# Attention in steps of two pairs, with PSUM tiles of one purpose each

## Chip, cores and metric

The kernel runs on one core of one Trainium2 chip. The metric is the device time of one execution in microseconds (us), as the median of several runs.

## What is computed

The reference is an attention with a window and a few sink positions, followed by two dense layers that keep the name "moe" from their source:

```python
scores = scale * q @ k.T                      # batch 2, 8 heads, 768 positions, 64 wide
keep = (pos_k < n_sink) | (0 <= pos_q - pos_k < window)       # n_sink 4, window 128
a = softmax(where(keep, scores, -1e9))
x = (a @ v), heads side by side               # 1536 rows x 512
h = maximum(x @ moe_w_in, 0);  y = (h * h) @ moe_w_out        # 512 -> 2048 -> 512
h = y @ moe2_w_in
out = (h * tanh(log1p(exp(h)))) @ moe2_w_out
```

## The kernel before, in words

**Tiles.** The 768 positions of each batch are cut into 6 tiles of 128 queries (12 tiles in all, numbered over both batches), and the 8 heads into 4 pairs. The unit of work is a pair of a tile: 48 pairs, numbered 0 to 47. The two heads of a pair (e = 0, 1) lie in partitions 0 to 63 and 64 to 127 of the transposed q and k. A tile with i >= 2 within its batch looks at 208 keys (`WIN`): each half of its query rows (64 rows, index h or r) has its own window of keys, and 16 sink keys (`SK`) are copied between the keys for that purpose by POOL (`sink_keys`, L334). Tile 0 of a batch uses 128 keys, tile 1 uses 256.

**Stages of a pair.** `prep` (L315) transposes q or k of a whole tile on TensorE (4 transposes of 128x128, shown as tr) into a PSUM tile of pool `ps_p`; DVE copies q to `qt`, ACT copies k to `kt`. `emit_s` (L365) computes the scores (s) of one pair, each head into a PSUM bank of its own from `ps_s`. `emit_max` (L380) adds the mask in place on DVE and takes the extreme of each row, one head at a time. `emit_exp` (L389) is the exponential on ACT with the row sums, from PSUM into the probability tile `pr`. `emit_rs` (L401) forms the reciprocals of the sums of two pairs on DVE (L407, L408), and `emit_norm` (L412) multiplies on POOL. `emit_t` (L418) transposes the probabilities of two pairs on TensorE (pt), 16 transposes of 64-row halves, into two banks of `ps_p`, one for each half of the rows; `evac_t` (L436) copies one bank at a time to `pts`, bank 0 on ACT and bank 1 on DVE. `emit_av` (L450) multiplies with v (av). `emit_x` (L477) copies a finished tile from PSUM on ACT, POOL rounds it to a high part (L481) and subtracts for the low part (L483); for the last two tiles DVE subtracts (`split_x`, L490).

**PSUM.** The eight banks: four for `ps_s`, three for `ps_p` (tr and pt alike), one for `ps_a` (av).

**Order.** The order of the work on each engine is written out by hand: the loop at L549 walks n from -3 to 52, one pair a turn. In turn n the scores and maxes of pair n+4, the exponentials of pair n+3, in even turns the reciprocals and normalisation of pairs n+2 and n+3, a `prep` of tile t+2 and the products of pairs n-4 and n-3, in odd turns the transposes of pairs n-1 and n are issued. SP issues all loads of the stage: a tile's q, k, v and `vx` (v rows of the shifted windows and of the sinks, `load_rest`, L292) are loaded three or four tiles ahead when j = 3. `PLAN` (L497) says in which turn which operation of the first three weight blocks is issued (a block is loaded, its words turned into 32-bit floats by ACT (head) and DVE (mid), and split into a high and a low part), and `IN_AT` (L503) when the first two input products of layer one are issued. A short prologue before the loop works on tile 0 in halves, with dummy matmuls (`keep_warm`, L527, shown as idle) on TensorE between.

**After the attention** the function `moe` (L615) runs both layers for all rows, in slots of 12 input matmuls (h) and 12 output matmuls (o, L634), with weight blocks converted on the way.

The lines that set the order around the change are these:

```python
        for n in range(-3, NPR + 5):
            at = {d: pairs[n + d] for d in range(-4, 5) if 0 <= n + d < NPR}
...
            if 4 in at and n > -3:
                emit_s(*at[4])
            if 3 in at and n > -3:
                emit_exp(*at[3])
```

## Time and profile before

| | |
|---|---|
| median of 3 runs | 620.19 us (619.1 to 620.61) |
| the profiled execution | 619.7 us |
| its span, first to last instruction | 617.9 us |
| TensorE matmul busy (PE) | 609.0 us, 99% of the span |
| weight loads (PEld) | 494.5 us, beside the matmuls |
| VectorE (DVE) | 454.5 us, 74% |
| ScalarE (ACT) | 351.0 us, 57% |
| GpSimd (POOL) | 70.1 us, 11%, all in the attention |
| granted TensorE clock, mean | 1.000 of full speed |
| first output matmul of the layers | at 95.80 us |

The shares are means over two very different stages: an attention of some 95 us in which all engines and the DMA engines work, and some 522 us of large matmuls. Names in the rows are those of the program's tiles; "out<-in" says what an instruction writes and reads, and a number in square brackets is idle time of the engine ahead of the instruction with what ended it.

### The profile page before, as it was taken

Reading aid. Unit: us, or ns where it says so; the run is one execution under the profiler, and the core shown is the slowest. Engines: PE = TensorE matmul, PEld = TensorE weight load, DVE = VectorE, ACT = ScalarE, POOL = GpSimd, SP = SyncE. Lnnn points to the kernel's source line nnn. Section 1 sums busy time; section 2 is a strip of 40 time slices with the busy share of each in tenths; the row PEclk is TensorE's granted clock in tenths of the full one; section 3 lists DMA queues with packets and bytes.
Section 4 is the critical chain, followed back from the end, with each engine's and each line's share of the span. In section 5 each row is a group of like instructions: output and inputs, shape, how many; then the busy total and the mean of one; then the engine's idle time right before and its main releaser. Section 6 shows DMA issues by size and latency. Waiting matters only on the chain.

```text
span 617.9 us, 10113 instructions
## 1 busy us (share of the span) xinstructions
PE 609.0 (99%) x3774; PEld 494.5 (80%) x3774; DVE 454.5 (74%) x951; ACT 351.0 (57%) x723; POOL 70.1 (11%) x101
## 2 busy tenths in 40 slices
PE   9999999999999999999999999999999999999996
PEld 6676677888888888888888888888888888888885
DVE  5897889998921111169898789999887788887784
ACT  4888876777743233367777655555444444454442
POOL 5788870000000000000000000000000000000000
PEclk9999999999999999999999999999999999999999
DMA  9998835666600000026666400000010000010001
GB/s 190 198 191 173 185 102 185 207 201 201 198 7 1 0 2 1 1 90 186 190 186 199 137 0 2 1 0 1 1 69 0 1 0 1 28 42 1 1 0 72
DMA packets 74904, 50.24 MB, mean 81 GB/s; under 512 B 52708, under 2 KB 69348, under 8 KB 74852
## 3 DMA queue, kind: packets, MB, share of 16 engines
q1 hardware_dynamic: 74560, 49.16, 29.0%
q8 instruction: 31, 0.51, 0.4%
q10 hardware_dynamic: 292, 0.39, 0.2%
q14 instruction: 21, 0.17, 0.1%
HBM read 46.40 MB, written 3.15 MB: 80 GB/s over the span
## 4 chain that ended last, share of the span: by engine, by line
PE 96%; DVE 2%; ACT 1%; issue 0%; DVEq 0%; ACTq 0%
PE o L634 42%; PE h L195 41%; PE s L373 4%; PE av L465 3%; PE tr L323 2%; PE pt L428 2%; PE idle L529 1%; DVE cv_a L148 0%; DVE cv_r L142 0%; ACT pr L396 0%; DVE cv_r L136 0%; DVE pts L443 0%; DVE qt L329 0%; DVE s L384 0%; DVE rs L408 0%
## 5 line engine op out<-in xcount | busy, mean ns | idle before, releaser
L195 PE MATMUL h<-xh,wil 128*128 128x512 f32 x384 | 102.9, 390 | 0.0
L195 PE MATMUL h<-xl,wih 128*128 128x512 f32 x384 | 102.6, 389 | 0.0
L195 PE MATMUL h<-xh,wih 128*128 128x512 f32 x384 | 102.6, 389 | 0.0
L209 DVE TENSOR_TENSOR gl<-h,gh 128x512 fp32r<-128x512 f32 x48 | 33.2, 691 | 89.3 <-ACT gh L206 89.3
L195 PEld LDWEIGHTS h<-xl,wih 128*128 128x128 f32 x384 | 72.1, 188 | 15.0
L195 PEld LDWEIGHTS h<-xh,wih 128*128 128x128 f32 x384 | 72.1, 188 | 15.0
L195 PEld LDWEIGHTS h<-xh,wil 128*128 128x128 f32 x384 | 71.9, 188 | 14.9
L634 PE MATMUL o<-gh,wol 128*128 128x512 f32 x192 | 74.8, 389 | 0.8 <-DVE wol L171 0.8
L702 ACT ACTIVATE e<-t,small 128x512 f32<-128x512 f32 x48 | 34.8, 725 | 70.7 <-DVE t L698 70.7
L634 PE MATMUL o<-gl,woh 128*128 128x512 f32 x192 | 74.7, 389 | 0.0
L634 PE MATMUL o<-gh,woh 128*128 128x512 f32 x192 | 74.7, 389 | 0.0
L204 ACT ACTIVATE h<-h 128x512 f32<-128x512 f32 x48 | 27.9, 582 | 77.5 <-PE h L195 77.5
L634 PE MATMUL o<-wol,gh 128*128 128x512 f32 x176 | 68.5, 389 | 0.0
L634 PE MATMUL o<-woh,gl 128*128 128x512 f32 x176 | 68.5, 389 | 0.0
L634 PE MATMUL o<-woh,gh 128*128 128x512 f32 x176 | 68.5, 389 | 0.0
L718 ACT CAST gh<-t 128x512 fp32r<-128x512 f32 x44 | 27.4, 623 | 46.1 <-PE o L634 42.7
L148 DVE SCALAR_TENSOR_TENSOR cv_a<-cv_a,cv_r 128x512 int32<-128x512 int32 x64 | 45.2, 706 | 6.2
L209 DVE TENSOR_TENSOR gl<-t,gh 128x512 fp32r<-128x512 f32 x44 | 30.4, 690 | 19.5 <-ACT gh L718 19.5
L396 ACT ACTIVATE pr<-s,nm 128x208 f32<-128x208 f32 (+2 forms) x96 | 40.5, 436 | 6.1 <-DVE nm L384 5.7
L416 POOL TENSOR_TENSOR pr<-pr,rs 128x416 f32<-128x416 f32 (+2 forms) x48 | 41.5, 885 | 15.0 <-DVE rs L408 10.4
L128 ACT ACTIVATE cv_a<-raw 128x512 f32<-128x512 f32 x63 | 42.4, 675 | 0.4 <-DMA raw<-in_moe_w_in_dram 0.2
L634 PEld LDWEIGHTS o<-gh,wol 128*128 128x128 f32 x192 | 36.0, 188 | 8.2 <-PE av L465 0.9
(100 smaller groups left out, 1004.1 us busy)
## 6 DMA issues: line engine op xcount, KB each, us to landing
raw<-in_moe_w_in_dram SPq DMA_DIRECT2D x32, 512.0 KB, 4.0
raw<-in_moe_w_out_dram SPq DMA_DIRECT2D x32, 512.0 KB, 4.3
vn<-in_v_dram SPq DMA_DIRECT2D x12, 256.0 KB, 5.1
qn<-in_q_dram SPq DMA_DIRECT2D x10, 256.0 KB, 4.4
kn<-in_k_dram SPq DMA_DIRECT2D x9, 256.0 KB, 4.8
vx<-in_v_dram SPq DMA_DIRECT2D x16, 128.0 KB, 4.3
out_dram<-ob SPq DMA_DIRECT2D x8, 256.0 KB, 2.4
kn<-in_k_dram SPq DMA_DIRECT2D x6, 128.0 KB, 3.0
```

The source lines that it names most:

```text
L128: nc.scalar.activation(out=self.a, in_=high_words, func=AF.Copy, scale=2.0**-112)
L148: nc.vector.scalar_tensor_tensor(out=ai, in0=ai, scalar=3, in1=self.r, op0=ALU.logical_shift_left, op1=ALU.bitwise_or)
L195: nc.tensor.matmul(ph, lhsT=w[a][:, d, :], rhs=x[:, d, :], start=(m == 0 and d == 0), stop=(m == 2 and d == NDC - 1),)
L204: nc.scalar.activation(out=ph, in_=ph, func=AF.Relu)
L209: nc.vector.tensor_tensor(out=gl, in0=x, in1=f32(gh), op=ALU.subtract)
L373: nc.tensor.matmul(banks[e][qs, 0:w], lhsT=qt[b, i][r, j, qs], rhs=kt[r, j, k0 : k0 + w], start=True, stop=True, skip_group_check=True,)
L396: nc.scalar.activation(out=pr[b, i][:, 2 * j + e, 0:w], in_=banks[e][:, 0:w], func=AF.Exp, bias=nm[:, e : e + 1], scale=-1.0, accum_out=sm ...
L416: nc.gpsimd.tensor_tensor(out=x, in0=x, in1=rs.to_broadcast([P, 2, w]), op=ALU.mult)
L465: nc.tensor.matmul(av[b, i][e * D : (e + 1) * D, j, qs], lhsT=x[0:kv, 2 * j + e, :], rhs=pts[0:kv, c, e, qs], start=(j == 0 and m == 0), s ...
L634: nc.tensor.matmul(acc[sp][t], lhsT=a, rhs=x, start=(fb == 0 and m == 0), stop=(fb == NFB - 1 and m == 2),)
L702: nc.scalar.activation(out=e, in_=t, func=AF.Ln, bias=two)
L718: nc.scalar.copy(g_tiles(n)[0], et[n][1])
```

## The change

The loop goes in steps of two pairs (n even, -2 to 52). The order within a step is written anew.

- PSUM: three banks for `ps_s`, two for the new pool `ps_t` (q and k transposes), two for `ps_p` (one tile, both row halves of pt), one for `ps_a`.
- The scores of two pairs share two banks: head e of both pairs in bank e, 256 columns each. The maxes and the exponentials go head by head: bank 0 for both pairs, then bank 1.
- `prep_rows` transposes q or k in halves of 64 rows, the halves into a bank each, issued directly ahead of pt; `place_rows` copies both, q and k alike, on DVE in the next step. The prologue and tile 1 keep `prep`.
- `evac_t` copies both banks of pt in one ACT instruction. `emit_x` copies on DVE, and POOL takes the low part of every tile.
- The first half of the rows takes its probabilities as columns 0 to 127 and 128 to 255 instead of 0 to 127 and 80 to 207, with v and `vx` rows to match: `vx` is 80 rows high and loaded by four transfers instead of five. The probability tiles are two fixed tiles whose columns from 208 on POOL zeroes at the start.
- k has four buffers instead of three and is loaded and transposed a tile earlier; loads are issued at j = 2. `PLAN` and `SINKS` are moved to even turns.

```diff
-    ps_s = att.enter_context(tc.tile_pool(name="ps_s", bufs=4, space=PSUM, reuse_waits="tile"))
-    ps_p = att.enter_context(tc.tile_pool(name="ps_p", bufs=3, space=PSUM, reuse_waits="tile"))
+    ps_s = att.enter_context(tc.tile_pool(name="ps_s", bufs=3, space=PSUM, reuse_waits="tile"))
+    ps_p = att.enter_context(tc.tile_pool(name="ps_p", bufs=1, space=PSUM, reuse_waits="tile"))
+    ps_t = att.enter_context(tc.tile_pool(name="ps_t", bufs=1, space=PSUM, reuse_waits="tile"))
...
+    def prep_rows(t, which):
+        if t >= len(tiles):
+            return
+        b, i = tiles[t]
+        src = (qn if which == "q" else kn)[b, i]
+        free = ps_t.tile([P, 2, 512], F32, tag="tr", name="tr")[:, :, 0 : 2 * P]
+        free = free.rearrange("p r (j q) -> p r j q", j=NPAIR)
+        for j in range(NPAIR):
+            for r in range(2):
+                rows = slice(r * HQ, (r + 1) * HQ)
+                nc.tensor.transpose(
+                    free[:, r, j, :], src[rows, 2 * j : 2 * j + 2, :].rearrange("p h d -> p (h d)"),
+                    ident[rows, rows],
+                )
+        if which == "q":
+            qt[b, i] = apool.tile([P, NPAIR, P], F32, tag="qt", name="qt", bufs=2)
+            dst = qt[b, i]
+        else:
+            dst = kt[:, :, kpos(i) : kpos(i) + P]
+        st["rows"] = (dst.rearrange("p j (r q) -> p j r q", r=2), free.rearrange("p r j q -> p j r q"))
+
+    def place_rows():
+        if "rows" in st:
+            nc.vector.tensor_copy(*st.pop("rows"))
+
...
-        return ((0, KV), (0, KV))
+        return ((0, P), (0, KV))
...
-    pr = {}
-
-    def emit_s(b, i, j):
+
+    def emit_s(b, i, j, banks):
         c0, w, _ = geom(i)
-        banks = [ps_s.tile([P, 512], F32, tag="s", name="s") for e in range(2)]
...
-    def emit_exp(b, i, j):
+    prs = [apool.tile([P, H, 2 * P], F32, name=f"pr{k}") for k in range(2)]
+    pr = {p: prs[m % 2] for m, p in enumerate(tiles)}
+
+    def emit_exp(b, i, j, heads=(0, 1)):
         w = geom(i)[1]
-        banks, nm = st.pop(("s", b, i, j))
+        banks, nm = st["s", b, i, j]
         sm, s = sum_at(b, i, j)
-        if j == 0:
-            pr[b, i] = apool.tile([P, H, 2 * P], F32, tag="pr", name="pr", bufs=2)
-        for e in range(2):
+        for e in heads:
...
-        banks = [ps_p.tile([P, 2, 2, 2, P // 2], F32, tag="pt", name="pt") for _ in range(2)]
+        banks = ps_p.tile([P, 2, 2, 2, 2, HQ], F32, tag="pt", name="pt")
...
-                            banks[r][:, s, c, e, :], pr[b, i][rows, 2 * j + e, o : o + P], ident[rows, rows]
+                            banks[:, r, s, c, e, :], pr[b, i][rows, 2 * j + e, o : o + P], ident[rows, rows]
                         )
-        pts = apool.tile([P, 2, 2, 2, P], F32, tag="pts", name="pts", bufs=2)
+        pts = apool.tile([P, 2, 2, 2, 2, HQ], F32, tag="pts", name="pts", bufs=2)
         for s, p in enumerate(group):
-            st["pts", p] = pts[:, s]
-        st["evac"] = [(group, banks[r], pts[..., r * D : (r + 1) * D], r) for r in range(2)]
-
-    def evac_t(eng=None):
...
+            st["pts", p] = pts[:, :, s]
+        st["evac"] = (group[0][1], banks, pts)
+
+    def evac_t():
+        if "evac" in st:
+            i, x, y = st.pop("evac")
+            c0 = 0 if i else 1
+            nc.scalar.copy(y[:, :, :, c0:], x[:, :, :, c0:])
...
-        whole = slice(0, P)
+        both, lo, hi = slice(0, 2), slice(0, 1), slice(1, 2)
         if i < 2:
-            parts = [(P, c, whole, vn[b, i - 1 + c]) for c in range(2) if i or c]
+            parts = [(P, c, both, vn[b, i - 1 + c]) for c in range(2) if i or c]
         else:
-            lo, hi = slice(0, HQ), slice(HQ, P)
             parts = [
-                (KV, 0, lo, vn[b, i - 1]), (P, 1, lo, vx[b, i][:, 0]),
+                (P, 0, lo, vn[b, i - 1]), (KV, 1, lo, vx[b, i][:, 0]),
                 (KV, 0, hi, vx[b, i][:, 1]), (P, 1, hi, vn[b, i]),
             ]
-        for m, (kv, c, qs, x) in enumerate(parts):
+        to = av[b, i][:, j].rearrange("p (r q) -> p r q", r=2)
...
-                    av[b, i][e * D : (e + 1) * D, j, qs], lhsT=x[0:kv, 2 * j + e, :],
-                    rhs=pts[0:kv, c, e, qs], start=(j == 0 and m == 0),
+                    to[e * D : (e + 1) * D, rs], lhsT=x[0:kv, 2 * j + e, :],
+                    rhs=pts[0:kv, rs, c, e], start=(j == 0 and m == 0),
...
-        nc.scalar.copy(x, av.pop((b, i)))
+        nc.vector.tensor_copy(x, av.pop((b, i)))
         nc.gpsimd.tensor_copy(hi, x)
-        if b * NB + i < len(tiles) - 2:
-            nc.gpsimd.tensor_tensor(out=lo, in0=x, in1=f32(hi), op=ALU.subtract)
-        else:
-            st["x"] = (x, hi, lo)
-
-    def split_x():
-        if "x" in st:
-            x, hi, lo = st.pop("x")
-            nc.vector.tensor_tensor(out=lo, in0=x, in1=f32(hi), op=ALU.subtract)
+        nc.gpsimd.tensor_tensor(out=lo, in0=x, in1=f32(hi), op=ALU.subtract)
...
-        0: {5: "load", 11: "head", 13: "mid_r1", 15: "mid_r2", 17: "mid_or", 19: "high low"},
-        2: {36: "load", 41: "head_pool", 44: "mid_r", 45: "mid_or", 46: "high low"},
-        1: {37: "load", 46: "head mid_r", 47: "mid_or", 48: "high low"},
+        0: {4: "load", 10: "head", 12: "mid_r1", 14: "mid_r2", 16: "mid_or", 18: "high low"},
+        2: {34: "load", 42: "head", 44: "mid_r mid_or", 46: "high low"},
+        1: {36: "load", 46: "head mid_r", 48: "mid_or high low"},
     }
 
     IN_AT = (46, 48)
-    SINKS = {n0 + 2 * (i - 2): i for n0 in (-1, NB * NPAIR - 3) for i in range(2, NB)}
+    SINKS = {n0 + 2 * (i - 2): i for n0 in (-2, NB * NPAIR - 4) for i in range(2, NB)}
...
+        load_tile(4, "k")
...
+        for x in prs:
+            nc.gpsimd.memset(x[:, :, WIN:], 0.0)
...
+        banks = ps_t.tile([P, 2, 512], F32, tag="tr", name="s")
+        emit_s(*pairs[0], [banks[:, e] for e in range(2)])
...
+        emit_s(*pairs[1], [ps_s.tile([P, 512], F32, tag="s", name="s") for e in range(2)])
...
-        for n in range(-3, NPR + 5):
-            at = {d: pairs[n + d] for d in range(-4, 5) if 0 <= n + d < NPR}
-            last = {d for d in at if at[d][2] == NPAIR - 1}
+        emit_exp(*pairs[1])
+        for n in range(-2, NPR + 6, 2):
+            at = {d: pairs[n + d] for d in range(-4, 6) if 0 <= n + d < NPR}
...
+            new = [at[d] for d in (4, 5) if d in at]
+            if new:
+                banks = [ps_s.tile([P, 2, 2 * P], F32, tag="s", name="s") for _ in range(2)]
+                for s, p in enumerate(new):
+                    emit_s(*p, [x[:, s] for x in banks])
+            for d in (-4, -3):
+                if d in at:
+                    emit_av(*at[d])
+            place_rows()
+            evac_t()
+            group = [at[d] for d in (2, 3) if d in at]
+            if n < 0:
+                heads = ps_p.tile([P, 2, 512], F32, tag="pt", name="tr")
+                for c, which in enumerate("qk"):
+                    prep(1, which, pt=heads[:, c])
+            elif group:
+                emit_rs(group)
+            for e in range(2):
+                for p in new:
+                    emit_max(*p, e)
+            if n < 0:
+                emit_rs(group)
+            for p in group:
+                emit_norm(*p)
+            if -3 in at and at[-3][2] == NPAIR - 1:
+                emit_x(*at[-3][:2])
+            for e in range(2):
+                for p in new:
+                    emit_exp(*p, (e,))
+            if new:
+                prep_rows(t + 2 + j // 2, "qk"[j // 2])
+            if 0 in at:
+                emit_t([at[0], at[1]])
+            if n < 0:
+                keep_warm(2 * WARM[3])
+            if n >= 0 and j:
                 load_tile(t + 4, "q", halves=1 + (t + 5 == len(tiles)))
-                load_tile(t + 4, "k", halves=1 + (t + 6 >= len(tiles)))
+                load_tile(t + 5, "k", halves=1 + (t + 7 >= len(tiles)))
                 load_tile(t + 3, "v")
                 load_rest(t + 3)
...
+                if n == IN_AT[fb] + 2:
                     ready[fb] = new_g(gpool)
                     relu_squared(early[fb], ready[fb][0])
-                if n == IN_AT[fb] + 2:
                     low_part(early[fb], *ready[fb])
```

## Rows read from the trace of the kernel before

**Rows 1.** The page of the kernel before, its first line.
```profile
span 617.9 us, 10113 instructions
```

**Rows 2.** Timeline of TensorE, around 95 us: start, us, engine, line, operation, idle.
```profile
95.80 0.47 PE L634 MATMUL o<-gh,wol 128*128 128x512 f32 x1 [0.79 <-DVE wol L171]
```

**Rows 3.** Windows: stretch, length, busy us and instructions by engine, clock, DMA share, GB/s.
```profile
20.00:40.00 20.00, 19.98 (x356) 14.00 (x352) 16.80 (x72) 17.74 (x64) 16.26 (x19) 1.00 0.98 197
```

**Rows 4.** Chain of waits, first 95 us: start, us, engine, tile, line, instructions.
```profile
10.09 0.59 PE tr L323 x4
10.68 0.22 PE idle L529 x2
10.90 0.38 PE s L373 x8
11.28 0.42 PE idle L529 x2
...
31.79 1.08 PE av L465 x32
32.87 0.51 PE s L373 x8
33.39 0.64 PE pt L428 x16
...
34.54 0.58 PE tr L323 x4
35.12 1.08 PE av L465 x32
```

**Rows 5.** Timeline of DVE, three stretches of the attention.
```profile
20.16 0.38 DVE L384 CUSTOM_DVE_ANT_0 s<-s,mask_w 128x208 f32<-128x208 f32 x1
...
37.13 0.37 DVE L384 CUSTOM_DVE_ANT_0 s<-s,mask_w 128x208 f32<-128x208 f32 x1
...
37.76 0.14 DVE L384 DVE_READ_ACCUMULATOR2_ANT nm<- 128x1 f32 x1
...
80.92 0.16 DVE L407 TENSOR_REDUCE rs<-sum 128x4 f32<-128x8 f32 x1 [0.17 <-ACT pr L396]
...
81.21 0.66 DVE L443 COPY pts<-pt 128x512 f32<-128x512 f32 x1
81.78 0.37 DVE L384 CUSTOM_DVE_ANT_0 s<-s,mask_w 128x208 f32<-128x208 f32 x1
```

**Rows 6.** Timeline of ACT, two stretches of the attention.
```profile
37.59 0.43 ACT L396 ACTIVATE pr<-s,nm 128x208 f32<-128x208 f32 x1 [0.67 <-DVE nm L384]
...
80.29 0.43 ACT L396 ACTIVATE pr<-s,nm 128x208 f32<-128x208 f32 x1
...
81.11 0.45 ACT L396 ACTIVATE pr<-s,nm 128x208 f32<-128x208 f32 x1
```

**Rows 7.** Groups by shape, first 100 us: busy us, mean ns, idle.
```profile
L443 ACT COPY pts<-pt 128x512 f32<-128x512 f32 x20 | 11.8, 588 | 3.6 <-PE pt L428 3.5
...
L396 ACT ACTIVATE pr<-s,nm 128x256 f32<-128x256 f32 x16 | 7.5, 477 | 1.6 <-DVE nm L384 1.6
...
L384 DVE CUSTOM_DVE_ANT_0 s<-s,mask 128x256 f32<-128x256 f32 x16 | 6.5, 449 | 2.4 <-PE s L373 2.3
...
L396 ACT ACTIVATE pr<-s,nm 128x128 f32<-128x128 f32 x16 | 5.7, 375 | 0.5 <-DVE nm L384 0.5
...
L384 DVE CUSTOM_DVE_ANT_0 s<-s,mask 128x128 f32<-128x128 f32 x16 | 4.4, 314 | 3.2 <-PE s L373 3.0
```

**Rows 8.** Timeline of POOL, 76 to 101 us.
```profile
77.04 0.61 POOL L481 CAST xh<-xf 128x512 fp32r<-128x512 f32 x1
...
78.97 1.72 POOL L416 TENSOR_TENSOR pr<-pr,rs 128x416 f32<-128x416 f32 x2
...
85.85 2.35 POOL L416 TENSOR_TENSOR pr<-pr,rs 128x416 f32<-128x416 f32 x2
```

**Rows 9.** DMA issues of the page: tiles, queue, count, KB each, us to landing.
```profile
vx<-in_v_dram SPq DMA_DIRECT2D x8, 96.0 KB, 5.1
```

63 lines of the change are left out of this document (9 added, 54 removed).

## The prediction

> **What bounds the kernel now.** I read the page first, then the windows, the chain of waits of the first 95 us, the timelines of each engine, and last the groups by shape. The span is 617.9 us [rows 1]. The execution took 619.7 us, 1.8 us more than its span and 0.5 us under the median of 620.19, so a difference in the span is carried to the median unchanged. At 95.80 us the first output matmul of the layers starts, after a wait of 0.79 for DVE [rows 2]. What follows it the change doesn't touch, so all that counts is when that matmul can start.
>
> Between 20 and 40 us TensorE is busy for 19.98 of 20 us at a granted clock of 1.00 (2.4 GHz), and the DMA engines for 0.98 [rows 3]. The chain is a row of TensorE pieces that touch: probability products (av) 1.08, scores (s) 0.51, transposes of probabilities (pt) 0.64, scores again, transposes of q or k (tr) 0.58, and at 35.12 the next av, 3.33 us after the one at 31.79 [rows 4]. Two pairs of heads cost 3.33 us, and TensorE alone sets it. DVE, ACT and POOL have room: the reader sees waits in brackets behind their rows [rows 5, 6].
>
> **What TensorE gains.** A piece has a fixed part. The scores take 0.38 us at 128 columns and 0.51 at 208 [rows 4]: 1.63 ns a column, 0.34 for 208, and 0.17 that doesn't depend on width. The two dummy matmuls show when it is paid: 0.22 us behind tr, which has their tile shape, and 0.42 behind s, which hasn't [rows 4]. That is 0.20 more, so I charge the 0.17 for each change of shape. In the changed step the scores of both pairs follow each other: 2 x 0.34 + 0.17 = 0.85 instead of 2 x 0.51. The q or k transposes become 8 of the form of pt's 16: 8/16 x (0.64 - 0.17) = 0.24, directly ahead of pt and in its shape, so without a fixed part of their own. The products stay at 1.08, the swapped halves (128 rows for 80, 80 for 128) change no count. Sum: 0.85 + 1.08 + 0.24 + 0.64 = 2.81 us. If nothing is shared it is 1.02 + 1.08 + 0.41 + 0.64 = 3.15. I take 2.81, since the dummies show both cases; 3.15 stays as an end.
>
> **What the order of DVE and ACT then costs.** Here another chain takes over. In the new loop DVE runs: copy of the last q or k transposes, sum and reciprocal (L407, L408) of the last step's pairs, four maxes of this step's. The sum waits for all four exponentials of the last step, and the maxes are queued behind it on DVE, though they need nothing from it. So a step can't be shorter than this ring:
> - From a bank's first max to its first exponential. With one pair in a bank it is 37.59 - 37.13 = 0.46 us [rows 5, 6]; two maxes take 0.63 until the second is read out [rows 5], 0.32 more than one: 0.78. The new program issues the maxes of both pairs of a bank ahead of both exponentials, and the bank is one tile. No row shows two engines in one bank, so the bounds are 0.46 (halves of a bank independent) and 0.78 (the bank handed over as a whole). I take 0.78.
> - Three more exponentials at (81.11 - 80.29) / 2 = 0.41 [rows 6]: 1.23.
> - From the last exponential's start to the sum: 80.92 - 80.29 = 0.63 [rows 5, 6].
> - Sum and reciprocal until DVE's next instruction: 81.21 - 80.92 = 0.29 [rows 5].
>
> Together 2.93 us, above TensorE's 2.81. What else moves fits inside. DVE has 2.93 - 4 x 0.32 - 0.29 = 1.36 us for its copies of q or k and, every second step, of x: 2 x 0.57 (from 81.21 to the next max at 81.78) [rows 5] = 1.14. ACT loses the copies of k and x and gains both banks of pt in one copy: 0.59 for one bank [rows 7], between 0.59 and 1.18 for two, I take 1.0; 4 x 0.41 + 1.0 = 2.64, room 0.29. POOL does four normalisations (1.72 a pair, at 78.97) and a split (78.97 - 77.04 = 1.93) a tile [rows 8]: 5.37 of 5.86 us. The DMAs: eight tiles lose one vx transfer of 96 KB each [rows 9], k is fetched a tile earlier into a fourth buffer, and SP issues a tile's loads one pair earlier, past nothing but each other and the one weight block behind them. DMA engines that are 0.98 busy [rows 3] could not feed a step 12% shorter with the same bytes for long, but bytes are dropped and k comes with a tile of lead, so I count nothing; without that cover the six steps of those 20 us would keep today's pace, 6 x 0.40 = 2.4 us. On POOL the copies of the first keys move up one pair and the two probability tiles are zeroed before the masks; both fall in its idle time, and only its next normalisation is queued behind.
>
> The Trainium skill has a rule on this ("PSUM — Partial Sum Buffer", section "PSUM bank collisions raise a hardware error"): two engines in the same bank and partitions at once are an error, even on different columns. By it the bank must be handed over as a whole and the step is 2.93; by the other bound the ring is 2.61 and the step TensorE's 2.81. No run here shows it yet.
>
> Tiles 0 and 1 of a batch have other widths. At 256 columns a max takes 449 ns and an exponential 477 [rows 7] against some 390 and 430 here: 2 x 0.06 + 4 x 0.045 = 0.30 more, 3.23. At 128, 314 and 375 [rows 7]: 2 x 0.08 + 4 x 0.06 = 0.40 less, 2.53.
>
> **The sum.** From pair 9's maxes (20.16, over 0.63 later at 20.8) to those of pair 47, the last (81.78, over at 82.4), the kernel now needs 61.6 us [rows 5]. Changed, these are 19 steps: 15 x 2.93 + 2 x 3.23 + 2 x 2.53 = 55.5. In four of them DVE or ACT also converts a weight block, operations of about 0.6 us where 0.2 to 0.3 is free: 0.8 more (0 to 1.5). So 56.3, a gain of 5.3.
>
> The fill loses. Three score banks instead of four make the second step's scores wait for pair 1's exponential; the transposes of tile 1, whose last stand at 10.09 to 10.68 now [rows 4], end about 1 us later, and the q copy of 0.6 stands ahead of the maxes on DVE. I put the first max of pairs 2 and 3 at 11.85 (11.3 to 12.9). Then 2.53 + 3.23 + 3.23 + four maxes of 0.32 bring pair 9 to 22.1 against 20.8: 1.3 lost (0.7 to 2.3).
>
> The tail, 82.4 to 95.80, I leave as it is: the first output matmul waits for DVE's last conversion [rows 2], DVE loses two splits and the bank copies, against which ACT's doubled copies hold up the transposes of the last pairs and the last split, now on POOL, has no reader soon. Bounds 1.5 either way.
>
> Gain: 5.3 - 1.3 = 4.0 us, 615.7 for the profiled execution, **616.2** for the median.
>
> **Rivals.** *TensorE stays the bound*: the halves of a bank are independent, the step is 2.81. That is 15 x 0.12 = 1.8 less, about 0.3 less in each of the four wide or narrow steps, 0.6 in the fill: 3.6, 612.6. Against it is the order of issue, for it only that no row shows the hand-over.
>
> *The change doesn't do what it says on TensorE*: the pieces keep their fixed parts and the step is 3.15. 15 x 0.22 = 3.3 more, 619.5. Against it are the 0.22 and 0.42 of the dummies, for it that no row has two score pieces in succession.
>
> *POOL becomes the bound*, the one that is slower: at 85.85 a pair of normalisations took 2.35 us [rows 8], beside conversions on DVE. If DVE's denser work did that in every step, a tile would need 2 x 2.35 + 1.93 = 6.63, a step 3.32, and 19 x 0.39 = 7.4 more gives 623.6. It decides once a pair costs over (5.86 - 1.93) / 2 = 1.97. Against it: in the attention proper the pair takes 1.72, and DVE's copies, which read PSUM, don't grow.
>
> A page of the Trainium skill speaks on the forecast's side against a large gain ("TensorEngine Tiling (Array Packing)", section "Performance Considerations"): tiling speeds TensorE up but not the emptying of PSUM, which may become the bound. By it the 0.52 us that TensorE saves a step would not all arrive; the ring above lets 0.40 of them through.
>
> **How the numbers follow.** A measurement of this kernel can tell about 0.3%, 1.9 us: faster is under 618.3, slower over 622.1. I give the ring of 2.93 a chance of 0.50 (0.45 faster, 0.05 same, its bounds reaching 613.5 to 619), TensorE's bound 0.13 (faster), the unshared pieces 0.22 (0.05 faster, 0.17 same), POOL 0.15 (0.02 same, 0.13 slower). Faster 0.63, same 0.24, slower 0.13. The range 612.8 to 620.8 leaves out POOL and about half of TensorE's case.
>
> **What would show it.** Right: four maxes in succession on DVE, and ahead of the next four a sum whose wait is put down to ACT's exponentials; steps of about 2.9 us; scores of 16 in about 0.85 us; q and k transposes and pt as one stretch of about 0.9; short TensorE waits in each step; ACT copies of about 1.0; the first output matmul near 91.7. Wrong: an exponential that starts before its bank's second max ends, steps of 3.1 or more with TensorE dense, normalisations over 0.98 us each, or TensorE waiting for q or k from DMA.

## The result, and the profile after it

The changed kernel is slower: 628.95 us, the median of five executions from 626.25 to 630.37, against 620.19 (619.1 to 620.73). The ratio is 1.014, with an interval of 1.0115 to 1.0166. The profiled execution took 626.25 us, 1.95 more than its span. Its page begins:

```profile
span 624.3 us, 10265 instructions
```

That is 6.4 more than before [rows 1]. TensorE's timeline shows that all of it lies ahead of the first output matmul [rows 2] (behind it come 522.0 us, before 522.1), and the windows show a TensorE that is busy for 18.24 of the 20 us from 20 to 40, where it was busy for 19.98 [rows 3] (the other rows belong to the stall below):

```profile
102.32 0.47 PE L650 MATMUL o<-gh,wol 128*128 128x512 f32 x1 [1.56 <-DVE wol L171]
```

```profile
20.00:40.00 20.00, 18.24 (x351) 13.63 (x350) 17.54 (x77) 16.75 (x58) 15.78 (x21) 1.00 1.03 201
...
48.50:50.50 2.00, 0.27 (x10) 0.13 (x6) 2.00 (x3) 0.72 (x1) 0.80 (x1) 1.00 1.04 230
50.50:52.50 2.00, 2.00 (x30) 1.70 (x34) 1.90 (x11) 1.01 (x6) 1.63 (x2) 0.54 0.05 11
52.50:54.50 2.00, 2.00 (x41) 1.67 (x42) 1.35 (x9) 1.52 (x6) 1.15 (x4) 0.60 0.00 0
54.50:56.50 2.00, 2.00 (x52) 1.55 (x48) 1.87 (x7) 2.00 (x9) 1.00 (x3) 1.00 0.37 85
```

Three stretches hold the loss. With the prediction's own marks (last max of pair 9 read out, last max of pair 47 read out, first output matmul):

| stretch | before | forecast | after |
|---|---|---|---|
| start to pair 9 | 20.8 | 22.1 | 23.8 |
| 19 steps, pair 9 to pair 47 | 61.6 | 56.3 | 63.4 |
| pair 47 to the first output matmul | 13.4 | 13.4 | 15.1 |

**TensorE's pieces came out as forecast.** Its timeline for one step of the changed kernel, which answers to [rows 4]:

```profile
36.04 0.46 PE L345 MATMUL tr<-ident,qn 64*128 64x64 f32 x8
36.49 0.71 PE L453 MATMUL pt<-ident,pr 64*128 64x64 f32 x16
37.13 1.03 PE L397 MATMUL s<-kt,qt 64*64 64x208 f32 x16
38.09 0.34 PE L484 MATMUL av<-pts,vn 128*64 128x64 f32 x4
```

Transposes of q and of probabilities take 37.13 - 36.04 = 1.09 here, with a hitch between them, and 0.89 in the step before (32.81 to 33.70); the forecast had 0.88. The scores of two pairs take 0.96 in this step (forecast 0.85); in most others a wait for a bank lies inside their row.

**The ring through the sum sets the step, and it is longer than forecast.** DVE and ACT in the step from 32.10 to 35.20 [rows 5, 6]:

```profile
31.81 0.16 DVE L432 TENSOR_REDUCE rs<-sum 128x4 f32<-128x8 f32 x1 [0.64 <-ACT pr L421]
...
32.10 0.36 DVE L408 CUSTOM_DVE_ANT_0 s<-s,mask_w 128x208 f32<-128x208 f32 x1
32.37 0.14 DVE L408 DVE_READ_ACCUMULATOR2_ANT nm<- 128x1 f32 x1
32.55 0.38 DVE L408 CUSTOM_DVE_ANT_0 s<-s,mask_w 128x208 f32<-128x208 f32 x1
32.85 0.14 DVE L408 DVE_READ_ACCUMULATOR2_ANT nm<- 128x1 f32 x1
32.85 0.42 DVE L408 CUSTOM_DVE_ANT_0 s<-s,mask_w 128x208 f32<-128x208 f32 x1
...
34.91 0.16 DVE L432 TENSOR_REDUCE rs<-sum 128x4 f32<-128x8 f32 x1
...
35.20 0.36 DVE L408 CUSTOM_DVE_ANT_0 s<-s,mask_w 128x208 f32<-128x208 f32 x1
```

```profile
33.11 0.43 ACT L421 ACTIVATE pr<-s,nm 128x208 f32<-128x208 f32 x1 [0.50 <-DVE nm L408]
...
34.35 0.43 ACT L421 ACTIVATE pr<-s,nm 128x208 f32<-128x208 f32 x1
```

The reader sees every link: first max to first exponential 33.11 - 32.10 = 1.01 (forecast 0.78), three exponentials 1.24 (1.23), last exponential to the sum 34.91 - 34.35 = 0.56 (0.63), sum to the next max 0.29 (0.29): 3.10 in place of 2.93. The sum at 31.81, in front of this step, waited 0.64 for ACT; the one at 34.91 shows no wait, since DVE's copies last until the same moment. Most of the 0.23 of the first link is a pause: the second max of a bank starts 0.18 after the read-out of the first began at 32.37, while the third, in the other bank, starts together with the read-out ahead of it (32.85). From read-out to read-out that makes 0.48, where the forecast charged 0.32 for a second max. The rest is a later start of the exponential, 0.26 behind the start of the last read-out (before: 0.17, from 37.42 to 37.59).

**One converted block stops the machine.** At step 18 ACT casts the high part of weight block 0 behind four exponentials, and DVE's low part waits for it. DVE and ACT there:

```profile
48.34 1.51 DVE L171 TENSOR_TENSOR wil<-cv_a,wih 128x512 fp32r<-128x512 f32 x1 [1.07 <-ACT wih L167]
49.77 0.68 DVE L358 COPY kt<-tr 128x512 f32<-128x512 f32 x1
50.37 0.14 DVE L432 TENSOR_REDUCE rs<-sum 128x4 f32<-128x8 f32 x1
```

```profile
47.27 0.44 ACT L421 ACTIVATE pr<-s,nm 128x208 f32<-128x208 f32 x1
...
47.68 0.63 ACT L167 CAST wih<-cv_a 128x512 fp32r<-128x512 f32 x1
```

Queued behind the waiting instruction are the copy of k and the sum. TensorE's next transposes need the copy, and the step took 5.62 us. TensorE, same rows as the windows above:

```profile
50.50 0.59 PE L345 MATMUL tr<-ident,qn 64*128 64x64 f32 x8 [1.74 <-DVE kt L358]
50.88 1.06 PE L453 MATMUL pt<-ident,pr 64*128 64x64 f32 x16
51.88 1.59 PE L397 MATMUL s<-kt,qt 64*64 64x128 f32 x16
```

Behind this wait TensorE's granted clock is 0.54 and 0.60 in two stretches of 2 us, close to the lower of its two levels (1.2 GHz), and pt takes 1.00 (50.88 to 51.88) instead of 0.64.

**The tail** lost its cover. TensorE's waits behind the last max are 3.45 us (0.82, 0.90, 0.17 and the 1.56 above); before they were 1.65 (0.19, 0.67 and 0.79). DVE, ACT and TensorE:

```profile
88.73 1.44 DVE L136 TENSOR_SCALAR cv_r<-raw 128x512 int32<-128x512 int32 x1
...
100.11 0.68 DVE L148 SCALAR_TENSOR_TENSOR cv_a<-cv_a,cv_r 128x512 int32<-128x512 int32 x1
101.48 0.69 DVE L171 TENSOR_TENSOR wol<-cv_a,woh 128x512 fp32r<-128x512 f32 x1 [0.69 <-ACT woh L167]
```

```profile
100.83 0.62 ACT L167 CAST woh<-cv_a 128x512 fp32r<-128x512 f32 x1 [3.33 <-DVE cv_a L148]
```

```profile
87.93 0.34 PE L484 MATMUL av<-pts,vn 128*64 128x64 f32 x4 [0.82 <-DVE xf L499]
...
90.03 0.71 PE L453 MATMUL pt<-ident,pr 64*128 64x64 f32 x16 [0.90 <-POOL xl L501]
```

The 1.56 ends a row of three: DVE's middle of weight block 1 (L148) is last in its queue, ACT's cast waits 3.33 for it, and DVE's low part (L171) for the cast. The 0.90 is put down to POOL's split of x, which these transposes don't read. Their own probabilities were ready at 87.58; the copy on ACT that empties their PSUM tile ran from 88.88 to 89.89, behind a conversion.

### The profile page after: what moved, and what is told of

The parts are those of the page before. It is cut to its first block, busy times and chain, and to the rows that moved or that the text cites. A ratio compares the mean times of both kernels' runs of the same rounds, so it can differ in the third digit from the quotient of the medians.

```text
span 624.3 us, 10265 instructions
## 1 busy us (share of the span) xinstructions
PE 608.1 (97%) x3852; PEld 496.2 (79%) x3852; DVE 459.8 (74%) x947; ACT 348.9 (56%) x702; POOL 71.7 (11%) x104
## 4 chain that ended last, share of the span: by engine, by line
PE 87%; DVE 7%; ACT 3%; issue 1%; POOL 0%; ACTq 0%; DVEq 0%; POOLq 0%
PE o L650 41%; PE h L194 41%; ACT pr L421 3%; DVE s L408 2%; PE s L397 2%; PE av L484 1%; PE idle L543 1%; DVE cv_r L136 1%; DVE wil L171 1%; DVE cv_a L148 1%; PE pt L453 1%; DVE nm L408 1%; DVE cv_r L142 0%; PE tr L324 0%; PE tr L345 0%
## 5 line engine op out<-in xcount | busy, mean ns | idle before, releaser
L194 PEld LDWEIGHTS h<-xh,wil 128*128 128x128 f32 x384 | 71.8, 188 | 15.5 <-DVE wil L171 0.5
L148 DVE SCALAR_TENSOR_TENSOR cv_a<-cv_a,cv_r 128x512 int32<-128x512 int32 x64 | 45.0, 702 | 6.4
L421 ACT ACTIVATE pr<-s,nm 128x208 f32<-128x208 f32 (+2 forms) x96 | 39.9, 428 | 16.6 <-DVE nm L408 15.4
L441 POOL TENSOR_TENSOR pr<-pr,rs 128x416 f32<-128x416 f32 (+2 forms) x48 | 41.4, 882 | 16.4 <-DVE rs L433 8.3
```

Source lines behind the costliest of these rows:

```text
L148: nc.vector.scalar_tensor_tensor(out=ai, in0=ai, scalar=3, in1=self.r, op0=ALU.logical_shift_left, op1=ALU.bitwise_or)
L194: nc.tensor.matmul(ph, lhsT=w[a][:, d, :], rhs=x[:, d, :], start=(m == 0 and d == 0), stop=(m == 2 and d == NDC - 1),)
L421: nc.scalar.activation(out=pr[b, i][:, 2 * j + e, 0:w], in_=banks[e][:, 0:w], func=AF.Exp, bias=nm[:, e : e + 1], scale=-1.0, accum_out=sm ...
L441: nc.gpsimd.tensor_tensor(out=x, in0=x, in1=rs.to_broadcast([P, 2, w]), op=ALU.mult)
```

## The experiments

In the table, from each kernel's profiled execution: **fill** is from the start of the first score matmul to the start of pair 9's last max, **steps** from there to the start of pair 47's last max, **tail** from there to the first output matmul. The first scores themselves start between 6.5 and 7.5 us, whatever the kernel, which is why the fill is counted from them. Ratios are to executions of the kernel before that ran beside each kernel (medians 619.28 to 620.19). A clean step is one with 208 keys and no weight conversion.

| kernel | median us | ratio, interval | fill | steps | tail |
|---|---|---|---|---|---|
| before | 620.19 | 1 | 13.0 | 61.6 | 13.7 |
| after | 628.95 | 1.0140, 1.0115 to 1.0166 | 16.4 | 63.4 | 15.4 |
| e1 | 627.04 | 1.0113, 1.0096 to 1.0130 | 17.9 | 62.8 | 15.8 |
| e2 | 624.56 | 1.0082, 1.0068 to 1.0097 | 17.5 | 60.9 | 15.4 |
| e3 | 626.16 | 1.0108, 1.0090 to 1.0126 | 16.4 | 64.9 | 15.0 |
| e4 | 626.33 | 1.0102, 1.0085 to 1.0119 | 17.9 | 60.7 | 17.5 |
| e5 | 623.65 | 1.0073, 1.0060 to 1.0086 | 17.1 | 59.5 | 14.7 |
| e6 | 624.09 | 1.0075, 1.0062 to 1.0088 | 16.6 | 60.5 | 15.5 |
| e7 | 624.13 | 1.0081, 1.0068 to 1.0094 | 16.4 | 60.9 | 13.8 |
| e8 | 620.55 | 1.0016, 1.0003 to 1.0029 | 15.1 | 58.8 | 15.8 |
| e9 | 623.06 | 1.0058, 1.0046 to 1.0070 | 15.3 | 61.5 | 16.5 |
| e10 | 627.30 | 1.0135, 1.0121 to 1.0150 | 16.5 | 63.5 | 15.5 |
| e11 | 619.23 | 1.0001, 0.9992 to 1.0010 | 15.1 | 58.8 | 14.2 |
| e12 | 619.99 | 1.0010, 1.0001 to 1.0019 | 14.8 | 59.2 | 14.7 |
| e13 | 618.21 | 0.9979, 0.9965 to 0.9993 | 13.9 | 59.0 | 14.2 |
| e14 | 618.44 | 0.9985, 0.9976 to 0.9994 | 13.8 | 59.0 | 14.2 |

**e1: the sum behind the maxes.**

```
-            elif group:
-                emit_rs(group)
             for e in range(2):
                 for p in new:
                     emit_max(*p, e)
-            if n < 0:
+            if group:
                 emit_rs(group)
```

> Sum and reciprocal are issued behind the four maxes of the step instead of ahead of them, nothing else. Theory A (the ring DVE, ACT, DVE sets the step: first max to first exponential 1.01, three exponentials 1.23, last exponential to sum 0.6, sum to max 0.2 to 0.3, together 3.10 us): the ring is broken, the clean step falls from 3.10 to between 2.85 and 2.95 us, where TensorE's pieces (0.96 + 1.08 + 0.89 = 2.93) or the wait of the scores for the bank of the step before end it; 15 steps by 0.15 to 0.25 give 2.3 to 3.8 us less than the changed kernel, 625 to 626.7. The maxes start without a wait for ACT. Theory B (the three score banks set the step: scores wait for the exponentials of the first bank): the step stays within 0.05 us of 3.10, the time within 1 us of 628.95, and the scores' wait for ACT stays at 0.4 a step or grows. Theory C (POOL sets it): the sum comes later, so the normalisations do, and TensorE waits for POOL in the transposes of the probabilities; the time rises by 1 to 3 us.

The clean steps fell to 2.98 to 3.07, no further, and the interval overlaps that of the changed kernel. DVE, TensorE and ACT of e1 in one clean step:

```profile
80.03 0.38 DVE L408 CUSTOM_DVE_ANT_0 s<-s,mask_w 128x208 f32<-128x208 f32 x1 [0.46 <-PE s L397]
...
83.03 0.38 DVE L408 CUSTOM_DVE_ANT_0 s<-s,mask_w 128x208 f32<-128x208 f32 x1 [0.44 <-PE s L397]
```

```profile
81.83 1.15 PE L397 MATMUL s<-kt,qt 64*64 64x208 f32 x16
82.92 0.34 PE L484 MATMUL av<-pts,vn 128*64 128x64 f32 x4
```

```profile
81.49 0.43 ACT L421 ACTIVATE pr<-s,nm 128x208 f32<-128x208 f32 x1
81.81 0.20 ACT L421 ACTIVATION_READ_ACCUMULATOR pr<-s,nm 128x1 f32 x1
```

The max now waits for scores, and these for a bank. With three banks the second bank of a step is the first of the step before. It is free when its second exponential has been read out, at 82.01; the scores end at 82.92 and the max starts at 83.03, 3.00 after the last one, although this step has no q or k transposes. Elsewhere POOL, which gets its sum later, now holds TensorE up (waits of 0.29 and 0.54 for POOL around 69 us, a step of 3.60). Theories A and C both hold in part, and B names the next cycle.

**e2: low part of block 0 at step 20.**

```
-        0: {... 18: "high low"},
+        0: {... 18: "high", 20: "low"},
```

> The low part of weight block 0 (DVE, which waits for ACT's high part) goes from step 18 to step 20, nothing else. Theory A (one DVE instruction that waits for ACT's cast behind four exponentials blocks the copy of k, the sum and with them TensorE, and the clock falls behind TensorE's idle time): the step that took 5.62 us (45.02 to 50.64) falls to 3.1 to 3.4, TensorE's wait of 1.74 for the copy of k goes, the granted clock of 50.5 to 54.5 us returns from 0.57 to over 0.9; 2.3 us less by the stall and 1 to 1.5 by the clock, so 3 to 4 us less than the changed kernel, 625 to 626. Theory B (the stall stands beside other work that would have taken the time anyhow, such as POOL's split that slows DVE's conversion to 1.5 us): the stall moves to step 20 and the time stays within 1 us of 628.95.

Theory A holds for the stall: the step took 3.10 and not 5.62, TensorE's clock is 1.00 from 48 to 60 us, and the interval lies below that of the changed kernel. Its sum isn't shown part by part: the median fell by 4.4 (forecast 3 to 4), the 19 steps of the profiled execution by 2.5, which is the stalled step alone. The conversion still takes 1.34, now behind the maxes: that step takes 3.36, the next of the same width 2.83, together 6.19, where the changed kernel took 6.17 for them at the lower clock.

**e3: middle of block 1 with its own block.**

```
-        1: {... 46: "head mid_r", 48: "mid_or high low"},
+        1: {... 46: "head mid_r mid_or", 48: "high low"},
```

> The last step of the middle of weight block 1's conversion (DVE) is issued at step 46, directly behind the other two of its own block, instead of at step 48, where it stands behind two more blocks' conversions and the low part of g; nothing else. Theory A (what ends the tail is DVE's low part of block 1, and it is late since its middle stands last in DVE's queue): ACT's high part, which waits 3.33 us, starts 2 to 3 us earlier, the wait of 1.56 us of the first output matmul goes, and it starts 1.3 to 1.6 us earlier; 627.4 by the median. Theory B (DVE as a whole is late in the tail, beside POOL's splits): the wait only moves to the next reader (g's low part, or the input products of the third block), and the time stays within 0.5 us of 628.95.

The wait of 1.56 went, and the tail is 0.4 shorter although the clock in it was at 0.50 from 92 to 94 us. The interval overlaps the changed kernel's: not decided by the time. The steps took 64.9, since the clock stayed at 0.50 to 0.55 until 58 us behind the same stall and a step there took 4.82 (3.30 in the changed kernel).

**e4: the three together**, the diffs of e1, e2 and e3.

> The three edits together: sum behind the maxes, low part of block 0 at step 20, middle of block 1 at step 46. Theory A (three separate losses: ring, blocked queue, tail): the gains add up, 2.3 to 3.8 + 3 to 4 + 1.5 = 6.8 to 9.3 us less than the changed kernel, 619.6 to 622.1, level with the kernel before. Theory B (one bound behind all of them, the three banks of scores or TensorE): the sum of the three single gains isn't reached by more than 2 us. Theory C (POOL): less than 3 us.

The gains didn't add up; e2 alone has the lower median, though the intervals overlap. The tail grew to 17.5: with the sum behind all maxes POOL's last normalisations end late, TensorE waits for them (1.14 and 0.91), and the clock falls behind the waits (0.53 and 0.61 between 94 and 98 us). TensorE of e4:

```profile
91.33 0.47 PE L453 MATMUL pt<-ident,pr 64*128 64x64 f32 x8 [1.14 <-POOL pr L441]
```

**e5: the sum between the banks**, with e2's edit.

```
-            elif group:
-                emit_rs(group)
             for e in range(2):
                 for p in new:
                     emit_max(*p, e)
-            if n < 0:
-                emit_rs(group)
+                if e == (n < 0) and group:
+                    emit_rs(group)
```

> On top of the edit that puts block 0's low part at step 20 (624.56 alone): sum and reciprocal between the maxes of the step's two banks, two maxes later than in the changed kernel and two earlier than behind all four. Theory A (bank cycle: with the ring broken, the second score bank of a step is the first of the step before, so a step can't be shorter than 1.03 from its first max to its first exponential + 0.94 for two exponentials + 0.9 for the scores that waited + 0.11 to the next max = 3.0 us): the clean step is 3.0, and the steps of 3.5 to 3.8 us that the sum behind all maxes gave go, since POOL gets its sum 0.7 us earlier; 15 steps by 0.12 give 1.8 less, 622 to 623.5. Theory B (the ring through the sum was the only bound): step 2.85 or less, 3 us less or more, under 621.5. Theory C (POOL): steps of 3.4 to 3.8 stay, the time is at or over 624.5.

Theory A: the clean steps are 2.98 to 3.02 but for the last (3.31), the step of 3.60 that POOL made is gone, and the 19 steps take 59.5. The median is 0.9 under e2's, just over A's 623.5, and the intervals overlap.

**e6: copies of the fill behind the maxes**, with e2's edit.

```
-                    prep(1, which, pt=heads[:, c])
+                    prep(1, which, pt=heads[:, c], later=heads_out)   # transposes only
...
+            if n < 0:                      # behind the maxes
+                for copy, dst, src in heads_out:
+                    copy(dst, src)
```

> On top of block 0's low part at step 20 (624.56 alone): in the fill, all eight transposes of tile 1's q and k are issued ahead of both copies, and the copies behind the maxes of pairs 2 and 3. Theory A (the tile that q's and k's transposes share makes k's wait 0.78 us for q's copy, and the copy holds back the first maxes by 1.1 us): the first max of the step starts at 10.9 instead of 11.4 to 12.2, TensorE's wait for the copy of q goes, the fill ends 0.8 to 1.2 us earlier, and with less idle time TensorE's clock holds more often in the fill (one fall there costs about 1.1 us in the profiled execution); 622.3 to 623.8. Theory B (three score banks set the fill): the steps behind it give the gain back, the maxes of pair 9 end no earlier than 23.5, the time stays within 0.7 us of 624.56.

Theory B by the time. The first max came 1.2 us earlier after the first scores, but the next scores waited 0.86 for ACT's copy of k, which now waited for DVE's copy of q out of the shared tile.

**e7: the tail in another order**, with e2's edit.

```
-        1: {... 46: "head mid_r", 48: "mid_or high low"},
+        1: {... 46: "head mid_r mid_or", 48: "high low"},
...
-    IN_AT = (46, 48)
+    IN_AT = (44, 48)      # at 44 ahead of emit_av
...
+            split_x()     # POOL's split of step 42's tile, behind the norms of 44
...
```

> On top of block 0's low part at step 20 (624.56 alone): in the tail the input products of block 0 are issued ahead of the products of pairs 40 and 41 (TensorE has them to do while it waits, as in the kernel before), POOL's split of the tile that ends at step 42 stands behind the last normalisation, and block 1's middle at step 46. Theory A (TensorE's waits of 0.8, 0.9 and 1.6 us in the tail come from the order there): these waits go or fall under 0.5 together, the first output matmul starts 13.3 to 14 us after the end of the last maxes instead of 15.4; 622.5 to 623.3. Theory B (DVE's conversions, which take 1.0 to 1.5 us beside POOL instead of 0.4 to 0.7, end the tail): the first output matmul still waits for the low part of block 1 for over 1 us, and the time is within 0.7 us of 624.56.

The tail fell by 1.7 to 13.8, with no wait at the first output matmul, as A has it; but 0.8 was given back behind it (its input products wait 0.65 for DVE's low part of the third block, which took 1.78 beside POOL's split), and the median isn't apart from e2's. TensorE of e7:

```profile
98.40 0.50 PE L661 MATMUL o<-gh,wol 128*128 128x512 f32 x1
...
102.31 1.20 PE L194 MATMUL h<-xh,wil 128*128 128x512 f32 x4 [0.65 <-DVE wil L171]
```

**e8: whole transposes in one bank, four banks of scores**, with e5's edits.

```
-    ps_s = ... bufs=3
+    ps_s = ... bufs=4
...
-        free = ps_t.tile([P, 2, 512], ...)     # 8 transposes of row halves
+        free = ps_t.tile([P, NPAIR, P], ...)   # 4 whole transposes, copied as they are
...
```

> On top of e5's two edits (low part at step 20, sum in the middle): the transposes of q and k go whole into one bank again, as in the kernel before, and the scores get the bank that this frees, four. Theory A (bank cycle and row-half transposes): the bank cycle is gone, and TensorE is the bound with 0.96 + 1.08 + 0.58 + 0.64 = 3.26 us in steps with a transpose; clean steps 3.2 to 3.3, the fill's steps fall from 3.4 to about 3.0, no wait of the scores for ACT; 15 steps by 0.25 lose 3.8 and the fill wins 1 to 1.5: 2 to 3 us more than e5. Theory B (sharing of shapes is worth nothing, the banks are all): steps of 2.9, faster than e5 by 1 to 2 us.

It came out against my theory A: 3 us faster than e5 by the median, not slower, and more than B's 2 (the profiled executions are 1.3 apart; e5's was its fastest). TensorE's step is longer, as A has it. The gain lies in the fill (15.1 for 17.1), less in the steps (58.8 for 59.5), and the tail gives 1.1 back, with a clock of 0.50 to 0.90 between 82 and 88 us. TensorE of e8:

```profile
58.25 0.66 PE L342 MATMUL tr<-ident,qn 128*128 128x128 f32 x4
58.84 0.71 PE L449 MATMUL pt<-ident,pr 64*128 64x64 f32 x16
59.48 0.93 PE L393 MATMUL s<-kt,qt 64*64 64x208 f32 x16
60.34 0.66 PE L480 MATMUL av<-pts,vn 128*64 128x128 f32 x8
```

The scores, which wait for no bank now, take 60.34 - 59.48 = 0.86 (forecast 0.85). Its clean steps are mostly 3.12, TensorE's 0.86 + 1.08 + 0.58 + 0.64 = 3.16, and some 2.4 to 2.6; e5's were 2.98 to 3.02.

**e9: e8 with the sum ahead of the maxes again.**

```
+            elif group:
+                emit_rs(group)
             for e in range(2):
                 for p in new:
                     emit_max(*p, e)
-                if e == (n < 0) and group:
-                    emit_rs(group)
+            if n < 0:
+                emit_rs(group)
```

> Part of e8 alone: block 0's low part at step 20, whole transposes of q and k in one bank, four banks of scores; the sum stays ahead of the maxes as in the changed kernel. Theory A (the ring through the sum and the bank cycle are two cycles of nearly one length, so that both must go): the ring holds the step at 3.10 to 3.17 and the fill's wide steps at 3.38; 622.5 to 624, most of the way to the 624.56 of the low part alone. Theory B (the banks alone made e8): 620 to 621, fill steps of 2.6 to 2.9.

Theory A. With e2, e5 and e8 this gives a square for the 19 steps, all with block 0's low part at step 20: 60.9 with ring and three banks, 59.5 without the ring, 61.5 with four banks and the ring, 58.8 without either. The medians are 624.56, 623.65, 623.06 and 620.55: only with both gone does most of it come back. In the steps the fourth bank helps only without the ring; with the ring, e9's gain is in the fill. Both kernels with four banks also have the whole transposes, so the two aren't told apart.

**e10: maxes in the order of the pairs**, so that the banks alternate, with e2's edit.

```
-            for e in range(2):
-                for p in new:
+            for p in new:
+                for e in range(2):
                     emit_max(*p, e)
```

> On top of block 0's low part at step 20 (624.56 alone): the four maxes of a step in the order of the pairs, so that the banks alternate; the exponentials stay in the order of the banks. Theory A (a max waits for the max before it in the same bank to be written): the pauses of 0.18 us in front of the second and fourth max go, four maxes take 1.3 instead of 1.56 us; a bank is now handed over behind the third max, so the first exponential starts 1.05 to 1.1 after the first max instead of 1.01, and the step stays at 3.10 to 3.2; time within 0.8 us of 624.56. Theory B (the pause belongs to the max itself, two reductions in halves of a bank): the pauses stay, now in front of other maxes.

The pauses went, as A has it, but its time (within 0.8 us) did not come: the kernel got 2.7 us slower. DVE and ACT of e10:

```profile
33.38 0.36 DVE L408 CUSTOM_DVE_ANT_0 s<-s,mask_w 128x208 f32<-128x208 f32 x1
...
33.65 0.42 DVE L408 CUSTOM_DVE_ANT_0 s<-s,mask_w 128x208 f32<-128x208 f32 x1
...
33.98 0.42 DVE L408 CUSTOM_DVE_ANT_0 s<-s,mask_w 128x208 f32<-128x208 f32 x1
34.31 0.14 DVE L408 DVE_READ_ACCUMULATOR2_ANT nm<- 128x1 f32 x1
```

```profile
34.57 0.44 ACT L421 ACTIVATE pr<-s,nm 128x208 f32<-128x208 f32 x1 [0.68 <-PE tr L345]
```

The first exponential starts 1.19 after the first max (1.01 before): it waits until the third max has been read out, since that is the bank's last (the bracket names TensorE's transposes, whose result this exponential doesn't read). The steps grew by just that, from 3.10 and 3.17 to 3.29 and 3.36. This shows the ring and its first link more plainly than e1 does.

In these steps each bank is one tile of the program, so e10 alone doesn't say which of the two makes the pause. The prologue of the changed kernel does. There pair 0 has one tile over two banks, and pair 1 has two tiles in two banks. DVE of the changed kernel, second max of either pair, and TensorE further on:

```profile
7.86 0.14 DVE L408 DVE_READ_ACCUMULATOR2_ANT nm<- 128x1 f32 x1
8.04 0.30 DVE L408 CUSTOM_DVE_ANT_0 s<-s,mask 128x128 f32<-128x128 f32 x1
...
9.43 0.14 DVE L408 DVE_READ_ACCUMULATOR2_ANT nm<- 128x1 f32 x1
9.43 0.33 DVE L408 CUSTOM_DVE_ANT_0 s<-s,mask 128x128 f32<-128x128 f32 x1
```

```profile
12.15 0.66 PE L324 MATMUL tr<-ident,kn 128*128 128x128 f32 x4 [0.78 <-DVE qt L330]
```

Pair 0 has the pause of 0.18, pair 1 has none, and in e8, where pair 0 has two tiles as well, its pause is gone (7.27). So it goes with the tile and not with the bank. The same holds for a wait between engines: in tile 1's tile q and k have a bank each, and k's transposes still wait 0.78 for DVE's copy of q; with a tile each (e14) they don't (10.67).

**e11 and e12: e8 with the tail repaired** (e7's edits, block 2 converted a step earlier, the low parts of the last two tiles on DVE); e12 also with the alternating maxes of e10.

```
...
+        2: {34: "load", 40: "head", 42: "mid_r", 44: "mid_or high", 46: "low"},
+        1: {36: "load", 44: "head", 46: "mid_r mid_or high", 48: "low"},
...
+        if t >= len(tiles) - 2:
+            nc.vector.tensor_tensor(out=lo, in0=x, in1=f32(hi), op=ALU.subtract)
```

> e8 (620.55) with the tail in another order: input products of block 0 at step 44 ahead of the products of the probabilities, conversion of block 2 one step earlier, block 1's middle together at step 46, POOL's split of the tile of step 42 behind the last normalisation, the low parts of the last two tiles on DVE as in the kernel before. Theory A (the tail's waits are its order): from the last max to the first output matmul 13.2 to 13.9 us instead of 15.8, no fall of TensorE's clock there; 618 to 619, a little under the kernel before. Theory B (the MoE's own conversions on DVE end it): the first output matmul comes earlier, but the next input products wait for it, and the time stays over 620.

> e11 with the maxes in the order of the pairs (banks alternate). Theory A (with ring and bank cycle gone, DVE's 0.36 us of pauses a step count where DVE also converts): steps with a conversion (3.4 to 3.8 us) fall by 0.2 to 0.3 each, the others stay; 0.5 to 1.2 us less than e11. Theory B (TensorE holds all steps, or the later hand-over of the first bank costs as much): within 0.4 us of e11.

e11 is level with the kernel before (A had it a little under); its tail fell from 15.8 to 14.2, in which the clock stayed up, as it had not in e8. In e12 the pauses are worth nothing: it is 0.8 above e11 (B allowed 0.4), with intervals that overlap, and its steps take 59.2 for 58.8. Without the ring DVE isn't what the steps wait for.

**e13 and e14: what was left of the fill.** e13 moves the three flag operations (L85 to L89) from step 2 to step 24; e14 also gives tile 1's q and k a tile each, and copies q behind the maxes.

```
-            if n == 2:
+            if n == 24:
                 fast_flag()
...
+                prep(1, "q", pt=heads[:, 0], later=heads_out)             # e14
+                prep(1, "k", pt=ps_t.tile([P, 512], F32, tag="tr", ...))  # e14
...
```

> e11 (619.23) with the three small flag operations on DVE, 1.35 us together, at step 24 instead of step 2, where the copy of k, and behind it TensorE and the next maxes, stand behind them. Theory A (they are on the fill's path): the step that took 3.96 us falls to about 2.7 to 3.0, the fill ends about 1 us earlier, and at step 24 DVE has the time; 618.0 to 618.6, under the kernel before. Theory B (DVE isn't what the fill waits for there, or step 24 loses as much): within 0.4 us of e11.

> e13 with tile 1's q and k transposed into two tiles instead of one, k's transposes without a wait for q's copy, and the copy of q behind the four maxes of pairs 2 and 3. Theory A (the shared tile): the first max of pairs 2 and 3 starts 0.9 to 1.1 us earlier after the first scores, TensorE's wait of 0.78 goes, the next scores start about 0.6 us earlier; the fill is 0.5 to 0.8 shorter than e13's, 617.4 to 618. Theory B (the next scores wait for both copies anyhow, and these now come later on DVE): the first maxes come earlier, the fill ends no earlier, time within 0.4 us of e13.

The step of 3.96 in the fill fell to 2.77 and the fill to 13.9. e13 is under both kernels, by 0.2% against the one before (0.9965 to 0.9993). e14 is level with it: the first max came earlier, the fill's end didn't, so the shared tile costs nothing there that counts.

## Why the prediction was wrong

Forecast 615.7 for the profiled execution, measured 626.25. The 10.5 us are the table's three differences: 1.7 in the fill, 7.1 in the steps, 1.7 in the tail.

- **TensorE's step of 2.81**: right. Pieces of 0.86 to 0.96, 1.08 and 0.89 make 2.83 to 2.93. The fixed part is shared (two pairs' scores take 0.86 in e8, not 2 x 0.51), and the rival with unshared pieces is out.
- **The ring**: the mechanism was right, down to the wait of the sum for ACT (0.64 us at 31.81). The term that failed is the first link, "0.78" from a bank's first max to its first exponential. The row it came from had two maxes in two tiles; on one tile there is a pause between them, and the link is 1.01, beyond both bounds (0.46 and 0.78). That it is handed over as a whole was right (e10). With 0.2 in 15 steps that is about 3 us. The four steps of other widths took 13.0 in place of 11.5; their maxes have the same pause, and two of them stand behind the stall. These two sums and the 2.5 of the next point make up the 7.1 of the steps.
- **"What else moves fits inside"** failed at block 0. The step costed the conversions by their durations (0.8 us) and named no wait. The wait of DVE's low part for ACT's cast is new in its place: the cast now stands behind four exponentials and the copy of k behind the low part. e2 shows 2.5 us in the steps and 0.6% of the time, clock included.
- **One ring was not the whole bound.** The prediction set the ring of 2.93 against TensorE alone. Behind the ring stands the cycle through three banks at 3.00 (e1, e5). I had counted the third bank in the fill and not in the steps. This is why breaking the ring returned so little, but it is no second cause of the miss: this cycle holds the same first link (1.03 in e1), and with the 0.78 of the forecast it would be 2.75, an estimate from e1's rows, under the ring of 2.93.
- **The fill**: its first max was right (12.01 for 11.85). The three steps behind it were not: 10.2 us (12.01 to 22.25) instead of 9.0, and the four maxes at the end took 1.56 instead of 1.28. The ring at 256 columns is 3.38 for 3.23 (15.43 to 18.81), and the scores of the first of these steps start only at 13.77. A fourth bank, with the whole transposes, brings 1.1 back (e9); where banks and ring are out of the way, the flag operations hold another 1.2 (e13).
- **The tail at nothing**: wrong by 1.7. "I leave as it is" overlooked that in the new order the input products stand behind the last transposes of the probabilities and no longer cover TensorE's waits, which grew by 1.8. e7 brings 1.7 back by three edits at once; which of them does it isn't separated, and 0.8 is lost again behind the first output matmul.
- **Rivals**: the slower end came, but not by POOL, whose pair still takes 1.72 in the steps without a conversion. TensorE as the only bound is out. DMA counted at nothing was right: no wait of TensorE for a transfer in these stretches.

No first exponential starts before its bank's last max was read out: at 33.11 behind 32.85 + 0.14 and in e10 at 34.57 behind 34.31 + 0.14. By the Trainium skill ("PSUM — Partial Sum Buffer", section "PSUM bank collisions raise a hardware error") two engines must not be in the same partitions of a bank at once, and these rows agree. They don't test the rule, though: the waits of this program go by its tiles, also where a tile spans two banks (the 0.78 at 12.15), and no run here lets two engines into one bank.

Left open is the share of the clock. The forecast carried a difference in the span to the median unchanged, and that failed too. Of the changed kernel's five executions the mean granted clock was 0.997 at 626.25 us, 0.990 at 628.13 and 628.95, 0.987 at 629.44 and 0.984 at 630.37; the kernel before stays at 0.998 to 1.000 in the executions beside e8. So the median is 2.7 us above the profiled execution, and a lower clock goes with it. No run held the clock and left the waits, so this share is read from the executions and not separated.

## What to carry to other kernels

Before two steps are folded into one, write down every cycle that the new order closes (through the sum, through the banks, through the one engine that converts), each with its length, and not only the longest: here three lay within some 0.3 us of one another, and removing one returned little (0.9 us of the median in e5, 1.5 in e9). Mark the links that two cycles share. Take the price of a link from a row with the same layout of tiles, or bound it upward. And for every instruction that waits for another engine, name what is queued behind it; one such wait cost 2.5 us, more than the 0.8 charged for all conversions by duration.

## What was not expected of the hardware

- Two reductions in succession on one PSUM tile have a pause of 0.18 us between them; on alternating tiles none (e10). The pause goes with the tile of the program, not with the bank (7.86 to 8.04 against 9.43); whether a wait in the program makes it, no row shows. With the ring gone it costs nothing (e12).
- TensorE's clock falls behind waits, but not in every execution: after one of 1.74 us the granted clock was 0.54 and 0.60 for 4 us in the changed kernel and 0.50 to 0.55 for 6 us in e3, whose steps took 1.5 us more. In the fill it fell in e2 (0.50 from 12 to 14 us) and in e1 and e4, and not in the changed kernel, whose fill has the same waits as e2's (0.96 and 0.78); the fill of e2 is then 17.5 instead of 16.4, 1.1 us for one fall.
- DVE's conversions beside POOL's work take 1.44 and 1.51 us instead of 0.41 and 0.69. The Trainium skill ("SBUF — State Buffer", section "Who interferes with whom") has DVE and POOL share a pair of ports as an exclusive lock, and a DVE instruction with two SBUF inputs contend with a POOL instruction that reads SBUF. The trace fits that: the low part that started at 48.34, inside POOL's split of 48.02 to 49.29, ended at 49.85, 0.56 behind it.
